# Three engines in program order instead of one, with the work dealt in smaller steps, in an attention and SwiGLU kernel

## The chip, the cores and the metric

The kernel runs on one core of a Trainium2 chip. The metric is device time in microseconds (us) from start to end of one execution; the median of the runs is taken. Nothing else runs on the core.

## The reference

```python
def _attn_ref(q, k, v):                 # 8 batches, 8 heads, 576 tokens, 64 values a head
    chunk, scale = 64, 1.0 / np.sqrt(64)
    q_c, k_c, v_c = (a.reshape(8, 8, 9, chunk, 64) for a in (q, k, v))
    scores = scale * np.matmul(q_c, k_c.transpose(0, 1, 2, 4, 3))
    scores = scores - np.max(scores, axis=-1, keepdims=True)
    attn = np.exp(scores)
    attn = attn / (np.sum(attn, axis=-1, keepdims=True) + 1e-09)
    return np.matmul(attn, v_c).reshape(8, 8, 576, 64)

def _moe_ref(x, w_gate, w_val, w_out, rms_g):   # x 4608 x 512; up to 1536, back to 512
    rms = np.sqrt(np.mean(x * x, axis=-1, keepdims=True) + 1e-06)
    xn = x / rms * rms_g
    g = xn @ w_gate
    silu = g * (1.0 / (1.0 + np.exp(-g)))
    return silu * (xn @ w_val) @ w_out
```

Each chunk of 64 tokens attends to itself. The heads are laid side by side to 4608 tokens of 512 values; these go through a norm and a gated up- and out-projection.

## The kernel before

The tokens go through in nine tiles of 512. Every operand of a projection is split into a high part (a copy rounded to the type that TensorE takes in one pass, on ScalarE) and a low part (operand less high part, on VectorE), and each product is the sum of three: high by high, high by low, low by high. So a matmul of 128x512 stands on TensorE for each of the three, and a split costs one ScalarE and one VectorE instruction.

**Tiles zero to two** are plain. In each, a loop over 12 feature blocks f makes the gate and the value product of block f (`up`, twelve matmuls each, L505), SiLU on ScalarE, the product with the value on VectorE, the split (`gated`), and then the out-projection of the block before (`down`, twelve matmuls, L540). In tiles one and two `half()` runs one step of a table of side work before `down` and one behind it.

**Tiles three to eight** are three pairs of tiles. A pair's projections use a scheme with seven block products P1 to P7 where eight would be due. `up_pair` runs for i = 0 to 5 over the seven products, each of two halves m (twelve matmuls together, L722); `after` turns the results into the gated block g: additions on VectorE, SiLU and copies on ScalarE, sums and products on GpSimd. Behind the seven, VectorE makes the operand tt and updates g in place (L761, L762). Then `down_pair` multiplies with the out weights in the order `DOWN`, each product for i = 0 to 5 (L911), with `finish` behind the last of a product. `split_next(n + 1)` splits the operand of the next product into gh and gl (L829, L830), one product ahead. The token operands of a pair (seven combinations of x, split as xp: L662, L663) are made by `x_sides`, the out weights of the seven products (side) by `out_sides` in tile two, the up weights' by `sides` in tile one; weights go through DRAM and come back through rings.

**The attention** of later tokens runs beside this, in units of 256 tokens, four to a pair of tiles (tile two carries the first pair's). From tile one on a unit (`unit_steps`) is: load q, k, v; scores (TensorE, L244) and softmax; the exponentials e turned in blocks of 32 by VectorE and stored to DRAM (away_e); read back as eT (L349); values (128 small matmuls of 64x64, L366); times the reciprocal sums rs, then the norm (squares summed on ScalarE, a power on GpSimd, a scale on ScalarE, L388); the result xu turned (L394) and stored (away_x); read back into x (L404). SyncE issues all of these transfers in one queue.

**What sets the order.** Work is dealt by tables: `UNIT_AT` and `UNIT_STEPS` in tile two, `PAIR_AT` and `PAIR_STEPS` in a pair give the step in which each part of a unit is emitted; `Steps` runs them. In tile zero a scheduler orders every engine. From tile one on TensorE runs in the order in which the code is written (`manual_schedule` with TensorE alone), while the scheduler still orders VectorE, ScalarE, GpSimd and SyncE: an instruction may be put ahead of others that are written before it, and `with urgent()` gives those on the path a priority. So the splits for the first products of an out-projection can be made long before it.

Of the kernel before, what the change touches and what calls it, by code (L numbers as in the profile page):

```python
# [17 lines left out]
P = 128  # L18
CH = 64
D = 64  # L20
H = 8
# [19 lines left out]
UNIT_STEPS = -2, 0, 1, 3, 5, 6, 7  # L41
FIRST_STEPS = -2, 0, 1, 3, 7, 8, 9
PAIR_STEPS = -4, 0, 3, 5, 8, 11, 13
PAIR_AT = 2, 12, 21, 31
# [24 lines left out]
def tile_chunk_attn_swiglu(  # L69
# [238 lines left out]
    def turned_softmax(i):  # L308
# [4 lines left out]
        for j in range(2):  # L313
            nc.vector.tensor_reduce(mx[:, j], st["s"][j], axis=AX.X, op=ALU.max)
            nc.vector.tensor_tensor(
                ev[:, j],
                st["s"][j].rearrange("p a (t k) -> p a t k", t=2),
                mx[:, j].rearrange("p a (o i) -> p a o i", i=1).broadcast_to([P, NPAIR, 2, Q]),
                op=ALU.subtract,
            )  # L320
        nc.scalar.activation(e, e, AF.Exp, scale=SCALE)
# [52 lines left out]
    def turned_norm(i):  # L374
        st = state.pop(i)
        if i % 2 == 0:

            state["xu", i // 2] = io.tile([P, 4, NDT, 2, Q], F32, tag="io", name="xu")
        xs = state["xu", i // 2].rearrange("p q a s d -> p s (q a) d")[:, i % 2]
        nc.vector.tensor_tensor(  # L380
            xs.rearrange("p (h b) d -> p h b d", b=2),
            st["o"].rearrange("p (h b d) -> p h b d", b=2, d=Q),
            st["rs"].rearrange("p h (o i) -> p h o i", i=1).broadcast_to([P, H, 2, Q]),
            op=ALU.mult,
        )

        spent = st["eT"].rearrange("p t h q -> p (t h) q")
        nc.scalar.mul(xs, xs, inv_rms(xs, spent))  # L388
# [125 lines left out]
    def gated(f, at, then):  # L514
# [14 lines left out]
        if 2 in at:  # L529
            then()  # L530
        with urgent():
# [41 lines left out]
    def out_sides(i, st):  # L573
# [6 lines left out]
        def join():  # L580
            w = st.tile([P, 2, DM], F32, tag="t1", bufs=1, name="wo")
# [75 lines left out]
    def x_side(p, src):  # L657

        t = xside[p] = big([P, 2, 2, TT], F32R, "xp")
        hi, lo = (t[:, i].rearrange("p k (n c) -> p k n c", c=2 * Q) for i in range(2))  # L660
        src = src.rearrange("p n k c -> p k n c")
        nc.scalar.copy(hi, src)  # L662
        nc.vector.tensor_tensor(lo, src, hi.bitcast(F32), op=ALU.subtract)  # L663

    xside = {}

    def x_sides(x1, x2, st):
# [3 lines left out]
        sub = ALU.subtract  # L671

        def scale(x, dts):
            for dt in dts:
                col = g_col[:, dt : dt + 1]
                nc.vector.tensor_scalar(x[:, :, dt], x[:, :, dt], col, None, op0=ALU.mult)

        def less(out, one, two):
            nc.vector.tensor_tensor(out, one, two, op=sub)

        def side_t1(p):
            x_side(p, got["t1"])

        def t1_first():
# [3 lines left out]
        got = {}  # L688
        first = [
            lambda: scale(x1, (0, 1)),  # L690
            lambda: scale(x1, (2, 3)),
        ]
        return first, [
            lambda: x_side(P1, b11),
            lambda: x_side(P2, b21),
            lambda: scale(x2, (0, 1)),
            t1_first,
            lambda: side_t1(P5),
            lambda: scale(x2, (2, 3)),
            lambda: less(got["t1"], b22, got["t1"]),  # L700
            lambda: side_t1(P6),
            lambda: x_side(P3, b22),
            lambda: less(b12, b22, b12),
            lambda: x_side(P7, b12),
            lambda: less(b21, got["t1"], b21),
            lambda: x_side(P4, b21),
        ]

# [116 lines left out]
    def split_g(src):  # L825
        gh = gp.tile([P, TT], F32R, name="gh")
        gl = gp.tile([P, TT], F32R, name="gl")
        with urgent():
            nc.scalar.copy(gh, src)  # L829
            nc.vector.tensor_tensor(gl, src, gh.bitcast(F32), op=ALU.subtract)  # L830
        return gh, gl

# [6 lines left out]
    def down_pair(t, gts, wos, step, more):  # L839
# [5 lines left out]
        def split_next(n):  # L845
            if n >= len(order):
                return
            p, i = order[n]
            g, tt = gts[i]
            src = {  # L850
# [3 lines left out]
            ready[n] = split_g(src)  # L854
# [11 lines left out]
        def finish(p, banks, kept):  # L866
            for m in range(2):
# [7 lines left out]
                elif p == P2:  # L875
                    o = tmp_tile("o")
# [18 lines left out]
        split_next(0)  # L895
        for n, (p, i) in enumerate(order):
# [9 lines left out]
            split_next(n + 1)  # L906
            gh, gl = ready.pop(n)
            w = wos[n // PER][:, n % PER]
            for k, (a, b) in enumerate(((0, gh), (1, gh), (0, gl))):
                for m in range(2):  # L910
                    nc.tensor.matmul(  # L911
                        banks[m][name],
                        w[:, a, m * P : (m + 1) * P],
                        b,
                        start=opens and i == 0 and k == 0,
                        stop=not (opens and p != P4) and i == NPR - 1 and k == 2,
                        skip_group_check=True,
                    )
            if i == NPR - 1:
                with urgent():  # L920
                    finish(p, banks, kept)
            step()

    def unit_steps(u, x):
# [3 lines left out]
        def first():  # L928
# [3 lines left out]
            for i in both:  # L932
                turned_softmax(i)

        def second():
            for i in both:
                turned_sum(i)
                turn(i)

        def third():  # L940
# [3 lines left out]
        def fourth():  # L944
            turned_values(u)
            for i in both:
                turned_norm(i)
# [5 lines left out]
            third,  # L953
            fourth,
# [54 lines left out]

    for t in range(PLAIN):  # L1010
        if t == 1:
            ordered = tc.manual_schedule(engines={mybir.EngineType.PE})
            ordered.__enter__()
            at = {}
# [3 lines left out]
            half = Steps(at)  # L1018
# [141 lines left out]
```

## Time and profile before

| | |
|---|---|
| runs | 930.78, 933.69, 937.71 us; median 933.69 |
| the profiled execution | 935.86 us; span of its instructions 934.0 us |
| granted TensorE clock, mean | 0.993 |
| TensorE / VectorE / ScalarE / GpSimd busy | 892.4 / 637.0 / 470.8 / 186.7 us |
| HBM traffic | 247 GB/s over the span |
| tiles zero and one | 0 to 258.4 us |
| tile two | 258.4 to 375.8 us |
| pair one: up, out | 375.8 to 505.8, to 567.0 us |
| pair two: up, out | 567.0 to 694.3, to 755.0 us |
| pair three: up, out (no attention beside it) | 755.0 to 870.6, to 934.0 us |

A row of the windows below gives a stretch, its length, the busy time of TensorE (with the number of instructions), its weight loads, VectorE, ScalarE, GpSimd, then the granted clock (1 is full), the share of the DMA engines and GB/s. A row of the timeline gives start, duration, engine, line, operation, result<-operands, tile, count, and in brackets how long the engine had waited and what ended the wait. SPq is SyncE's queue. Line numbers of the profile before are those of the kernel above; those of the changed kernel are other ones, since it has lines more.

### The profile page before, as it was taken

What the parts mean: (1) busy time and instruction counts of PE and PEld (TensorE: products, weight loads), DVE (VectorE), ACT (ScalarE), POOL (GpSimd) and SP (SyncE); (2) the same over time, 40 slices, a digit from 0 to 9 for tenths busy, and PEclk for the clock granted to TensorE, in tenths of its full rate; (3) what the DMA queues carried; (4) which work ended last, traced back from release to release, by engine and by line L of the source; (5) the groups of instructions that cost most, each with busy time, mean ns of one, the idle gap of its engine ahead of it and who ended that gap; (6) DMA issues with size and microseconds to landing.
All of it is one profiled execution on the core that took longest, in us unless ns stands there. A gap on an engine that the chain in (4) does not pass through costs nothing.

```text
span 934.0 us, 17571 instructions
## 1 busy us (share of the span) xinstructions
PE 892.4 (96%) x6828; PEld 726.1 (78%) x6828; DVE 637.0 (68%) x1065; ACT 470.8 (50%) x779; POOL 186.7 (20%) x161
## 2 busy tenths in 40 slices
PE   5699989999999989999998999999999999999997
PEld 4478868888888778888886888888877888888786
DVE  5899983654578783975775996666859954333775
ACT  4989853443456543744453654354636632322453
POOL 0100012224300000143333001443320013332201
PEclk9999999999999999999999999999999999999999
DMA  8688998778876766677796686777777675345801
GB/s 343 243 316 303 331 325 281 244 252 249 294 288 230 229 183 202 250 276 262 237 323 241 240 331 210 283 260 241 267 273 258 241 273 229 135 153 206 340 23 69
DMA packets 85795, 231.85 MB, mean 248 GB/s; under 512 B 8912, under 2 KB 45264, under 8 KB 71504
## 3 DMA queue, kind: packets, MB, share of 16 engines
q1 hardware_dynamic: 85712, 230.72, 70.3%
q8 instruction: 54, 0.88, 0.4%
q14 instruction: 29, 0.24, 0.1%
HBM read 167.25 MB, written 63.44 MB: 247 GB/s over the span
## 4 chain that ended last, share of the span: by engine, by line
PE 76%; issue 7%; ACT 6%; DVE 6%; POOL 2%; DMA 1%; SPq 0%; DVEq 0%; ACTq 0%; POOLq 0%
PE ps_c L722 11%; PE ps_a L722 11%; PE ps_b L722 10%; PE ps_g L505 7%; PE acc L540 7%; PE ps_v L505 7%; PE ps_b L911 5%; PE ps_d L722 5%; PE ps_c L911 4%; PE ps_d L911 3%; PE ps_a L911 3%; PE ps_o L366 2%; PE ps_s L244 2%; DVE gl L830 1%; ACT w L157 1%
## 5 line engine op out<-in xcount | busy, mean ns | idle before, releaser
L722 PE MATMUL ps_b<-xp,wr 128*128 128x512 f32 x432 | 106.0, 395 | 0.0
L722 PE MATMUL ps_c<-xp,wr 128*128 128x512 f32 x432 | 104.6, 391 | 0.0
L505 PE MATMUL ps_g<-xh,parts 128*128 128x512 f32 x288 | 98.1, 400 | 5.9 <-ACT sg L523 5.1
L722 PE MATMUL ps_a<-xp,wr 128*128 128x512 f32 x432 | 103.5, 390 | 0.0
L505 PE MATMUL ps_v<-xh,parts 128*128 128x512 f32 x288 | 96.0, 393 | 0.0
L722 PEld LDWEIGHTS ps_b<-xp,wr 128*128 128x128 f32 x432 | 81.7, 190 | 17.4
L722 PEld LDWEIGHTS ps_a<-xp,wr 128*128 128x128 f32 x432 | 80.9, 188 | 16.9
L722 PEld LDWEIGHTS ps_c<-xp,wr 128*128 128x128 f32 x432 | 80.6, 188 | 17.0
L540 PE MATMUL acc<-parts,gh 128*128 128x512 f32 x288 | 90.8, 396 | 0.0
L829 ACT CAST gh<-g 128x512 fp32r<-128x512 f32 x72 | 44.6, 623 | 51.8 <-DVE gl L830 21.0
L505 PEld LDWEIGHTS ps_g<-xh,parts 128*128 128x128 f32 x288 | 55.0, 191 | 19.5 <-ACT sg L523 6.4
L505 PEld LDWEIGHTS ps_v<-xh,parts 128*128 128x128 f32 x288 | 54.7, 190 | 11.5
L540 PEld LDWEIGHTS acc<-parts,gh 128*128 128x128 f32 x288 | 53.5, 189 | 11.6 <-ACT parts L182 0.2
L801 POOL TENSOR_TENSOR g<-u,u 128x512 f32<-128x512 f32 x18 | 23.2, 1289 | 185.8 <-ACT u L769 72.1
L830 DVE TENSOR_TENSOR gl<-g,gh 128x512 fp32r<-128x512 f32 x72 | 49.3, 700 | 12.2 <-ACT gh L829 11.9
L505 PE MATMUL ps_g<-xl,parts 128*128 128x512 f32 x144 | 57.0, 396 | 0.0
L540 PE MATMUL acc<-parts,gl 128*128 128x512 f32 x144 | 56.4, 392 | 0.0
L505 PE MATMUL ps_v<-xl,parts 128*128 128x512 f32 x144 | 56.4, 392 | 0.0
L791 POOL TENSOR_TENSOR p<-p,p 128x512 f32<-128x512 f32 x36 | 46.9, 1318 | 42.8 <-DVE p L790 33.5
L769 ACT ACTIVATE p<-p 128x512 f32<-128x512 f32 x36 | 22.6, 632 | 64.4 <-POOL p L791 61.2
L433 POOL TENSOR_TENSOR ri<-ss,mhalf 128x1 f32<-128x1 f32 x32 | 19.6, 623 | 173.6 <-DVE ss L431 173.5
L527 DVE TENSOR_TENSOR sg<-ps_v,sg 128x512 f32<-128x512 f32 x36 | 24.7, 686 | 42.0 <-PE ps_v L505 35.0
(141 smaller groups left out, 1794.9 us busy)
## 6 DMA issues: line engine op xcount, KB each, us to landing
wr<-wsd SPq DMA_DIRECT2D x63, 1024.0 KB, 6.8
wo<-osd SPq DMA_DIRECT2D x30, 1024.0 KB, 7.8
raw<-w_up_dram SPq DMA_DIRECT2D x12, 1024.0 KB, 9.6
vt<-v_dram SPq DMA_DIRECT2D x18, 512.0 KB, 5.2
wsd<-parts SPq DMA_DIRECT2D x18, 512.0 KB, 7.0
qt<-qT_dram SPq DMA_DIRECT2D x17, 512.0 KB, 4.9
kt<-kT_dram SPq DMA_DIRECT2D x17, 512.0 KB, 5.8
away_e<-e SPq DMA_DIRECT2D x28, 256.0 KB, 2.4
```

Of the source, the lines that this page charges most:

```text
L244: nc.tensor.matmul(st["s"][j][c * CH : (c + 1) * CH, pr], st["q"][rows, pr, tok : tok + CH], st["k"][rows, pr, tok : tok + CH], start=True ...
L433: nc.gpsimd.tensor_tensor(ri, ss, mhalf, op=ALU.pow)
L505: nc.tensor.matmul(ps, a[f][:, cols], b[dt], start=(dt == 0 and i == 0), stop=(dt == NDT - 1 and i == 2),)
L527: nc.vector.tensor_tensor(sg, pv, sg, op=ALU.mult)
L540: nc.tensor.matmul(acc[s], a[:, cols], b, start=(f == 0 and i == 0), stop=(f == NF - 1 and i == 2),)
L722: nc.tensor.matmul(ps, w[:, a, m, cols], xp[:, b, kt], start=start and kt == 0 and i == 0, stop=stop and kt == 1 and i == 2, skip_group_ch ...
L769: nc.scalar.activation(t, t if src is None else src, AF.Silu)
L791: nc.gpsimd.tensor_tensor(kp["p5"], kp["p1"], kp["p5"], op=add)
L801: nc.gpsimd.tensor_tensor(g[:, 0, 1], kp["u2"], kept[0]["u2"], op=mult)
L829: nc.scalar.copy(gh, src)
L830: nc.vector.tensor_tensor(gl, src, gh.bitcast(F32), op=ALU.subtract)
L911: nc.tensor.matmul(banks[m][name], w[:, a, m * P : (m + 1) * P], b, start=opens and i == 0 and k == 0, stop=not (opens and p != P4) and i ...
```

## The change

From tile two on TensorE, ScalarE and VectorE run in the order in which the code is written (`IN_ORDER`); GpSimd and SyncE keep the scheduler. A unit has eleven steps in place of seven: the softmax of the two halves, the exponentials, the turns, the norm, its root and its scale are steps of their own, and the power of both halves is one instruction on two columns. The token operands are made in more and smaller steps, their scale by rms_g goes from VectorE to ScalarE, and those of the last four products (P3, P6, P7, P4) are split in the first steps of the stage that uses them. Three of the six `out_sides` move from tile two to tile one. In tile two a step runs between gh and gl (`between`). In `down_pair` gh is made two products ahead and gl one, and the last of each product finishes its half m = 0 first.

```diff
+PAIR_AT = 3, 12, 22, 31
+PAIR_STEPS = -4, 0, 1, 3, 4, 5, 8, 9, 10, 11, 13
+UNIT_STEPS = -2, 0, 0, 1, 1, 3, 5, 6, 6, 7, 8
+IN_ORDER = {mybir.EngineType.PE, mybir.EngineType.Activation, mybir.EngineType.DVE}
...
+    def turned_norm(u):
...
+            nc.scalar.activation(spent, xv[:, s], AF.Square, accum_out=ss[:, s : s + 1])
+    def turned_root(u):
+        ss = state["ss", u]
+        nc.vector.tensor_scalar(ss, ss, 1.0 / DM, 1e-6, op0=ALU.mult, op1=ALU.add)
+        ri = state["ri", u] = small.tile([P, 2], F32, name="ri_u")
+        nc.gpsimd.tensor_tensor(ri, ss, mhalf.broadcast_to([P, 2]), op=ALU.pow)
+    def turned_scale(u):
...
+            nc.scalar.mul(xv[:, s], xv[:, s], ri[:, s : s + 1])
...
+        if between is not None:
+            between()
         with urgent():
             nc.vector.tensor_tensor(gl, sg, gh.bitcast(F32), op=ALU.subtract)
...
-                nc.vector.tensor_scalar(x[:, :, dt], x[:, :, dt], col, None, op0=ALU.mult)
+                nc.scalar.mul(x[:, :, dt], x[:, :, dt], col)
...
+        late = [
+            [lambda: less(got["t1"], b22, got["t1"]), lambda: high(P3), lambda: high(P6)],
+            [lambda: low(P6), lambda: less(b12, b22, b12), lambda: low(P3), lambda: high(P7)],
+            [lambda: low(P7), lambda: less(b21, got["t1"], b21), lambda: high(P4)],
+            [lambda: low(P4)],
+        ]
...
-        with urgent():
-            nc.scalar.copy(gh, src)
-            nc.vector.tensor_tensor(gl, src, gh.bitcast(F32), op=ALU.subtract)
...
+        def split_high(n):
+            if n < len(order):
+                gh = tmp.tile([P, TT], F32R, tag="tmp", name="gh")
+                nc.scalar.copy(gh, source(n))
+                ready[n] = [gh]
...
+        def split_low(n):
...
+            gl = gp.tile([P, TT], F32R, name="gl")
+            nc.vector.tensor_tensor(gl, source(n), ready[n][0].bitcast(F32), op=sub)
...
-        split_next(0)
+        split_high(0)
+        split_high(1)
+        split_low(0)
...
-            split_next(n + 1)
+            split_high(n + 2)
+            split_low(n + 1)
...
-            for k, (a, b) in enumerate(((0, gh), (1, gh), (0, gl))):
-                for m in range(2):
...
+            todo = [(m, k) for k in range(3) for m in range(2)]
             if i == NPR - 1:
-                with urgent():
-                    finish(p, banks, kept)
+                todo.sort()
+            for m, k in todo:
...
+            for i in range(OUT_FIRST):
+                for k, f in enumerate(out_sides(i, st, "ab", 3)):
+                    at.setdefault(7 + 6 * i + k, []).append(f)
...
+            ordered.__exit__(None, None, None)
...
+            ordered = tc.manual_schedule(engines=IN_ORDER)
+            ordered.__enter__()
...
+            g = gated(f, CONVS[f % 2], conv_step, half if t == 2 else None)
```

**VectorE around the first pair's out-projection.** Before, in row order; the first piece lies inside the up stage, the second at its end. p1 less ps_d is the end of P4 (two halves), g<-g is the update of the last block, xu is the last unit's turn, gl are the low parts of the out-projection's operands, the number behind the name tells the tiles apart (g_4026 is the block of i = 0, g_4227 of i = 1, g_4503 of i = 2).

```order
L762 TENSOR_TENSOR g_4026<-g_4026 128x512
L830 TENSOR_TENSOR gl_5474<-g_4026,gh_5473 128x512
L778 TENSOR_TENSOR u2_4294<-ps_b_4280,p1_4242 128x512
L778 TENSOR_TENSOR u2_4296<-ps_b_4287,p1_4244 128x512
L784 TENSOR_TENSOR g_4227<-ps_a_4235,c11_4312 128x512
L830 TENSOR_TENSOR gl_5482<-g_4227,gh_5481 128x512
```

```order
L803 TENSOR_TENSOR p1_5269<-p1_5269,ps_d_5453 128x512
L762 TENSOR_TENSOR g_5254<-g_5254 128x512
L394 STREAM_TRANSPOSE xu_5418<-xu_5418 128x1024
L803 TENSOR_TENSOR p1_5271<-p1_5271,ps_d_5460 128x512
L830 TENSOR_TENSOR gl_5495<-g_4503,gh_5494 128x512
L663 TENSOR_TENSOR xp_5568<-x_127,xp_5568 128x1024
L830 TENSOR_TENSOR gl_5505<-g_4750,gh_5504 128x512
```

The same place in the changed kernel, whose blocks i = 0, 1, 2 are g_3989, g_4199, g_4475 and whose gl is L881:

```order
L829 TENSOR_TENSOR p1_5225<-p1_5225,ps_d_5414 128x512
L829 TENSOR_TENSOR p1_5227<-p1_5227,ps_d_5421 128x512
L787 TENSOR_TENSOR tt_5207<-g_5210 128x512
L788 TENSOR_TENSOR g_5210<-g_5210 128x512
L881 TENSOR_TENSOR gl_5440<-g_3989,gh_5436 128x512
L881 TENSOR_TENSOR gl_5448<-g_4199,gh_5438 128x512
L411 STREAM_TRANSPOSE xu_5385<-xu_5385 128x1024
L881 TENSOR_TENSOR gl_5461<-g_4475,gh_5446 128x512
L881 TENSOR_TENSOR gl_5471<-g_4716,gh_5459 128x512
```

The low parts of i = 0 and i = 1 have moved from the up stage to behind P4's two halves, tt and the update of g.

**ScalarE at the same place.** p5 and p1 are SiLUs (P7, P4), xu<-xu,ri the scale of the norm, gh the high parts, xp a token operand. Before:

```order
L769 ACTIVATE p5_5289<-p5_5289 128x512
L388 ACTIVATE xu_5418<-xu_5418,ri_5423 128x16x32
L388 ACTIVATE xu_5418<-xu_5418,ri_5430 128x16x32
L769 ACTIVATE p1_5269<-p1_5269 128x512
L662 CAST xp_5568<-x_127 128x1024
L829 CAST gh_5494<-g_4503 128x512
L829 CAST gh_5504<-g_4750 128x512
```

In the changed kernel:

```order
L795 ACTIVATE p5_5256<-p5_5256 128x512
L795 ACTIVATE p1_5225<-p1_5225 128x512
L405 ACTIVATE xu_5385<-xu_5385,ri_u_5410 128x16x32 x2
L874 CAST gh_5436<-g_3989 128x512
L874 CAST gh_5438<-g_4199 128x512
L874 CAST gh_5446<-g_4475 128x512
```

The first two gh, made in the up stage before, now stand behind P4's SiLU and the two scales.

**SyncE's queue in tile two**, at the third unit. e is stored to away_e and read back as eT, x comes back from away_x of the unit before. Before:

```order
L349 DMA eT<-away_e_3320 32x2x256 x2
L397 DMA away_x_3358<-xu 128x1024
L349 DMA eT<-away_e_3320 32x2x256 x2
L349 DMA eT<-away_e_3327 32x2x256
L214 DMA vt<-v_dram 128x1024
L404 DMA x<-away_x_3358 32x4x256 x4
L349 DMA eT<-away_e_3327 32x2x256 x3
```

In the changed kernel:

```order
L355 DMA eT<-away_e_3361 32x2x256 x4
L355 DMA eT<-away_e_3368 32x2x256 x2
L414 DMA away_x_3433<-xu 128x1024
L355 DMA eT<-away_e_3368 32x2x256 x2
L217 DMA vt<-v_dram 128x1024
```

The four reads of x, which stood ahead of the last three of eT, come behind all eight now.

More of the change, by code (lines that the diff above doesn't have):

```diff
@@ L512, in up, with gated @@
         return ps
-    def gated(f, at, then):
+    def gated(f, at, then, between=None):
         pg = up(wgh, wgl, f, "ps_g")
@@ L670, in x_sides, with views, high, low @@
         b11, b21, b12, b22 = x1[:, :, :2], x1[:, :, 2:], x2[:, :, :2], x2[:, :, 2:]
-        sub = ALU.subtract
+        got = {}
+        src = {P1: lambda: b11, P2: lambda: b21, P5: lambda: got["t1"], P6: lambda: got["t1"]}
+        src.update({P3: lambda: b22, P7: lambda: b12, P4: lambda: b21})
+        def views(p):
+            t = xside[p]
+            hi, lo = (t[:, i].rearrange("p k (n c) -> p k n c", c=2 * Q) for i in range(2))
+            return hi, lo, src[p]().rearrange("p n k c -> p k n c")
+        def high(p):
+            xside[p] = big([P, 2, 2, TT], F32R, "xp")
+            hi, _, x = views(p)
+            nc.scalar.copy(hi, x)
+        def low(p):
+            hi, lo, x = views(p)
+            nc.vector.tensor_tensor(lo, x, hi.bitcast(F32), op=ALU.subtract)
         def scale(x, dts):
@@ L931, in first, with second, away, back @@
                 scores(i, sc)
+            turned_softmax(both[0])
+        def second():
+            turned_softmax(both[1])
             for i in both:
[L933 to L940, printed above, removed]
+                turned_exp(i)
+        def away(i):
+            turned_sum(i)
+            turn(i)
+        def back():
             for i in both:
                 turn_back(i)
-        def fourth():
+        def values():
             turned_values(u)
-            for i in both:
-                turned_norm(i)
+            turned_norm(u)
         return [
@@ L952, in unit_steps @@
             second,
-            third,
-            fourth,
+            lambda: away(both[0]),
+            lambda: away(both[1]),
+            back,
+            values,
+            lambda: turned_root(u),
+            lambda: turned_scale(u),
             lambda: turn_x(u),
@@ L1095, in tile_chunk_attn_swiglu @@
                     at.setdefault(max(PAIR_AT[n] + PAIR_STEPS[k], 0), []).append(f)
-            first, both = x_sides(x, x2, st)
-            for n, f in enumerate(first):
-                at.setdefault(PAIR_AT[1] + PAIR_STEPS[-1] + 4 + n, []).append(f)
-            for n, f in enumerate(both):
-                at.setdefault(7 * NPR + 6 + 5 * n // 2, []).append(f)
+            one, two, late = x_sides(x, x2, st)
+            for n, f in enumerate(one[:2]):
+                at.setdefault(PAIR_AT[1] + PAIR_STEPS[-1] + 2 + n, []).append(f)
+            for n, f in zip(X_AT, one[2:] + two[:1] + two[4:] + two[1:4]):
+                at.setdefault(7 * NPR + n, []).append(f)
+            early = {n: list(todo) for n, todo in enumerate(late)}
         step = Steps(at)
```

148 lines of the change are left out of this document (69 added, 79 removed).

## The prediction

> **What bounds the kernel now.** I read the busy table, then TensorE's waits, then the timeline around each wait.
>
> ```profile
> PE 892.4 (96%) x6828; PEld 726.1 (78%) x6828; DVE 637.0 (68%) x1065; ACT 470.8 (50%) x779; POOL 186.7 (20%) x161
> ...
> 406.90 1.48 PE L366 MATMUL ps_o<-vt,eT 64*32 64x64 f32 x128
> 408.31 3.02 PE L722 MATMUL ps_c<-xp,wr 128*128 128x512 f32 x12
> 411.17 1.07 PE L722 MATMUL ps_b<-xp,wr 128*128 128x512 f32 x4
> ```
>
> TensorE has 96%, and no edit takes a matmul away. Twelve wide matmuls take 2.86 us here (408.31 to 411.17), 2.72 without the 0.14 of the switch, so 0.227 each; a burst of attention values takes 1.41 (406.90 to 408.31). The change can win or lose only what TensorE idles. Tiles zero and one keep their scheduler, so I look from 258 us on. Three losses stand there. **Tile two:**
>
> ```profile
> 258.40:375.80 117.40, 113.72 (x1202) 92.52 (x1202) 83.58 (x178) 60.04 (x101) 5.24 (x8) 0.99 0.69 221
> ...
> 307.85 0.27 PE L366 MATMUL ps_o<-vt,eT 64*32 64x64 f32 x2 [0.33 <-DMA eT<-away_e]
> 309.00 1.94 PE L366 MATMUL ps_o<-vt,eT 64*32 64x64 f32 x126 [0.88 <-DVE rs L326]
> 330.70 2.42 PE L366 MATMUL ps_o<-vt,eT 64*32 64x64 f32 x126 [1.55 <-DMA eT<-away_e]
> 337.34 0.50 PE L505 MATMUL ps_g<-xh,parts 128*128 128x512 f32 x1 [0.59 <-ACT sg L523]
> ...
> 327.57:330.98 3.41, 1.77 (x12) 1.00 1.11 277
> 330.98:334.40 3.42, 3.29 (x126) 0.52 0.64 231
> ```
>
> 36 groups of twelve (97.9 us) and four units of about 2.5 (10.0) are 107.9 of the 117.4, so 9.5 are lost. Waits with a name are 3.35: the eT tiles, which come back from DRAM late, and a late silu. After the idle window from 327.57 the next 3.42 us were granted 0.52 of the clock, which costs 1.6.
>
> **The start of each paired out-projection**, here pair two; the last up product begins at 691.55, the out-projection at 694.27:
>
> ```profile
> L829 ACT CAST gh<-g x2: 619/620/620, 573.3 to 599.1; 128x512 fp32r<-128x512 f32 x2
> L830 DVE TENSOR_TENSOR gl<-g,gh x2: 693/693/693, 573.9 to 599.7; 128x512 fp32r<-128x512 f32 x2
> ...
> 690.15 1.28 DVE L380 TENSOR_TENSOR xu<-ps_o,rs 128x512 f32<-128x512 f32 x2
> 691.55 2.88 PE L722 MATMUL ps_d<-xp,wr 128*128 128x512 f32 x12
> 693.97 1.32 ACT L388 ACTIVATE xu<-xu,ri 128x512 f32<-128x512 f32 x2
> 694.27 1.07 PE L911 MATMUL ps_a<-gh,wo 128*128 128x512 f32 x4
> 694.39 1.29 POOL L791 TENSOR_TENSOR p<-p,p 128x512 f32<-128x512 f32 x1
> 697.08 0.69 DVE L762 TENSOR_TENSOR g<-g 128x512 f32<-128x512 f32 x1 [2.97 <-POOL g L795]
> 697.69 1.24 DVE L394 STREAM_TRANSPOSE xu<-xu 128x1024 f32<-128x1024 f32 x1
> 699.43 0.68 DVE L830 TENSOR_TENSOR gl<-g,gh 128x512 fp32r<-128x512 f32 x1
> 700.16 0.74 PE L911 MATMUL ps_a<-gl,wo 128*128 128x512 f32 x2 [1.62 <-DVE gl L830]
> 702.99 0.74 PE L911 MATMUL ps_a<-gl,wo 128*128 128x512 f32 x2 [1.17 <-DVE gl L830]
> ...
> PE ps_a L911 <- DVE gl L830: 6.0, 7, 1.6
> ```
>
> The first two splits were made over 90 us ahead, in the up stage. The third comes only after VectorE has waited for GpSimd (697.08) and turned a tile (697.69). All such waits sum to 6.0; seven of them, about 0.17 longer from start to start (a matmul is booked 0.39 but spaced 0.227), make 7.2. **A stall with no engine behind it**, in the last burst of pair one, and the clock around it and around pair two's start:
>
> ```profile
> 498.52 0.31 PE L366 MATMUL ps_o<-vt,eT 64*32 64x64 f32 x1 [2.03 <-issue]
> ...
> 494.82:498.24 3.42, 1.67 (x129) 1.00 1.01 422
> 498.24:501.65 3.41, 3.13 (x8) 0.52 1.01 428
> ...
> 699.62:703.04 3.42, 1.72 (x7) 1.00 1.00 333
> ```
>
> With the half clock behind it this one costs 2.3 + 1.6 = 3.9.
>
> **The change part by part.** *Tile two in program order.* The eT pieces are no longer queued behind the four loads of x, which wait for their own DRAM trip; only the store away_x still stands between them. From the end of an up product E:
>
> ```profile
> L349 SPq DMA_DIRECT2D eT<-away_e x32: 302/425/1075, 273.1 to 344.2; - x32
> ...
> DMA to landing us min/median/max: 1.8/2.7/5.2
> ...
> L527 DVE TENSOR_TENSOR sg<-ps_v,sg 128x512 f32<-128x512 f32 x12 | 8.2, 684 | 12.2 <-PE ps_v L505 8.4 <-issue 3.7
> ```
>
> the product sg (0.7, perhaps 0.3 late), the turn (1.24, as at 697.69), four issues of about 0.42 and the landing (2.7) give E + 6.6, up to E + 9.1 with the longest landing. TensorE comes to the burst after a down product (2.72), scores (1.1) and an up product (5.44): E + 9.3; for the last unit, which has no scores ahead, E + 8.2. So the waits go with a margin of 1.6 to 2.7. I count -5.5: 3.35 of waits, 1.6 of clock, 0.5 of the bursts' slow flow; bounds -3.3 (waits alone) and -8.4 (all but the switches between kinds of matmul, 8 times 0.14).
>
> Three out_sides move to tile one:
>
> ```profile
> L598 DVE TENSOR_TENSOR side<-wo,side x24: 370/419/426, 277.0 to 360.2; 128x256 fp32r<-128x256 f32 x24
> ```
>
> each takes eight VectorE passes over 128x256, about 0.42 like this one, and one over 128x1024, by the token split's 1.2 below: 4.6. I found no stall in tile one with such work as its cause, and count 0. The squares' sum to the scale, one power for a pair instead of two, and the scale by g on ScalarE run beside matmuls; ScalarE is busy half of the time: 0, unless the power is long (rival three).
>
> *Splits further ahead.* gh is made two products ahead, but gl stays one ahead, and in program order the first gh and gl now come after all of the last up product. In pair two's times: the two norms end at 690.0 (values end 688.7, 1.28); the half m=0 of P7 ends 690.2, its sum on VectorE (0.69) 690.9; m=1 likewise 692.3. GpSimd:
>
> ```profile
> L433 POOL TENSOR_TENSOR ri<-ss,mhalf 128x1 f32<-128x1 f32 x24 | 13.8, 588 | 137.7 <-DVE ss L431 137.7
> L470 POOL TENSOR_TENSOR ri_u<-ss_u,mhalf x2: 1616/2779/3942, 83.5 to 126.6; 128x2 f32<-128x2 f32 x2
> L769 ACT ACTIVATE p<-p 128x512 f32<-128x512 f32 x36 | 22.6, 632 | 64.4 <-POOL p L791 61.2 <-DVE p L803 2.3
> ...
> 398.63 1.29 POOL L807 TENSOR_TENSOR g<-p,p 128x512 f32<-128x512 f32 x1
> 398.69 1.78 DVE L762 TENSOR_TENSOR g<-g 128x512 f32<-128x512 f32 x1
> ```
>
> two sums of 1.3 to 693.6, the power to 694.2 (0.59, nearest to the 24 rows of this stage; 3.9 is the other end), the product to 695.5. ScalarE: silu of P4 to 694.25, the two scales (1.32) to 695.6, the first gh (0.62) to 696.2. TensorE, due at 694.27, starts 2.0 late and has four matmuls (0.9) until it needs gl, at 697.15. VectorE: P4's second half to 695.0, tt to 695.7, then the update of g. GpSimd takes up its next product in the same moment, and with that beside it this update took 1.78 at 398.69: 697.45; the first gl ends 698.1, another 0.95 late. Together 3.0. Pair three has no unit, no scales: gh 0.7 late, gl 1.7 more, 2.4. So -7.2 go and 3.0 + 3.0 + 2.4 = +8.4 come (bounds: 4.5 if GpSimd's next product waits and gh is early; 11 if the turn that follows adds its 1.24 as well).
>
> And the clock: a window with 1.77 or 1.67 us busy of 3.41 was followed by 0.52, one with 1.72 was not (699.62). A stall of 2.0 and one of 0.95 within 3.9 us leave a window about half idle in some 3 of 4 positions. I take it in pairs one and two: +3.2 (0 to 4.8). [...]
>
> *Pair starts in the up stage.* P6's low part must now be ready at 8.4 after the first product:
>
> ```profile
> L663 DVE TENSOR_TENSOR xp<-t,xp 128x1024 fp32r<-128x1024 f32 x6 | 7.3, 1218 | 0.0
> ```
>
> the second product ends at 5.44, silu 0.6, the product g 0.7, the split 1.2: 7.95. It fits by 0.45; +0.5 for three pairs (0 to 1.5).
>
> *The last out-projection finishes m=0 three matmuls earlier:*
>
> ```profile
> 928.42 0.61 PE L911 MATMUL ps_d<-gl,wo 128*128 128x512 f32 x2
> 928.92 1.29 DVE L890 TENSOR_TENSOR p<-p,ps_d 128x512 f32<-128x512 f32 x2 [1.67 <-PE ps_d L911]
> ```
>
> so only one of the two subtractions stands behind the last matmul: -0.6.
>
> *The stall at 498* belongs to TensorE's own stream, which is nearly the same: no row says whether it falls on the burst again. Half of 3.9, -1.9 (0 to -3.9).
>
> **Sum**, on the profiled span of 934.0: -5.5 - 7.2 + 8.4 + 3.2 + 0.5 - 0.6 - 1.9 = -3.1, so 930.9; its execution took 935.86, 1.9 more. The median shown is 933.69, less 3.1: **930.6**.
>
> **Rivals.** [...] *Two, the starts are cheap:* if gh and gl come with the lower bound of 4.5 and no half clock, tile two gives all 8.4 and the stall at 498 goes, the sum is -8.4 - 7.2 + 4.5 - 0.6 - 3.9 = -15.6: 918. For it: only GpSimd's order makes the update late. Against: VectorE waited 2.97 for that product before. *Three, slower: the power over two columns takes 3.9*, as once at 126. ScalarE, in order, then stands 3.3 longer ahead of the scale: both starts +6.6; in tile two the silu behind it comes about 1 late in each of four units, +4; copies of P1 in the up stage, +2: 943. It decides from about 2 us on. Against it: no single power took over 1.1 from 258 on. *Four, slower: eT lands after 9.3:* 2 us late and a half clock each in four units, 14.4 in place of the waits gone, 930.6 + 5.5 + 14.4 = 950; it needs landings over 5.4, and 5.2 was the longest. *Five, the order leads as before* and tile two keeps its waits: 936.
>
> **How the numbers follow.** Forecast 0.40, rival one 0.15, two 0.25, three 0.07, four 0.04, five 0.09. Within 1% (924.4 to 943.0, about what a measurement of this kernel can tell from no change) lie the forecast, one and five, less 0.05 for forecasts with the 498 stall gone and two cheap starts: 0.58. Faster 0.30, slower 0.12 (three lies on the border). The range, 918 to 940, leaves out three and four and half of two.
>
> **What would show it.** In the profile after: no eT wait in tile two; a wait of about 2 on gh and about 1 on gl at each out-projection's first products; VectorE's update of g waiting for GpSimd just ahead; a window at 0.52 behind it; the tail 0.6 shorter. The forecast is wrong if the first gl is ready when the out-projection starts, if powers take over 2 us, or if values still wait.

## The result: 5% slower

The changed kernel takes 983.3 us (median of 977.08, 981.23, 985.36 and 987.09) against 933.77: a ratio of 1.051, 95% interval 1.0474 to 1.0547. The forecast was 930.6, its range ended at 940. The profiled execution is the fastest of the four (977.08).

The busy table of the changed kernel, then three windows of TensorE alone: tile one before, then tiles one and two of the changed kernel. A row gives the stretch, its length, TensorE's busy time with the number of matmuls, the granted clock, DMA share and GB/s:

```profile
PE 903.4 (93%) x6828; PEld 733.5 (75%) x6828; DVE 645.4 (66%) x1027; ACT 463.7 (48%) x787; POOL 180.0 (18%) x147
```

```profile
154.30:258.10 103.80, 103.80 (x818) 1.00 0.79 255
149.70:271.20 121.50, 110.23 (x818) 0.94 0.76 243
271.20:395.30 124.10, 114.41 (x1202) 0.96 0.60 192
```

TensorE has the same 6828 matmuls, and no other engine is busy more than 8.4 us longer; the time is idle time and half clock (windows of 3.41 that were granted 0.50 to 0.53). The stages from first matmul to first matmul, in us, of every kernel run here (one profiled execution each; pair three with the tail; tile zero took 150 to 156 in all of them and is left out, 149.7 in the changed kernel, 154.3 before):

| | median / before of its runs | tile one | tile two | pair one | pair two | pair three |
|---|---|---|---|---|---|---|
| before | 933.77 | 103.8 | 117.3 | 191.3 | 189.6 | 177.5 |
| changed | 983.3 / 933.77 | 121.5 | 124.1 | 201.3 | 197.3 | 181.2 |
| e2, all out_sides in tile two | 973.83 / 934.43 | 103.8 | 130.8 | 203.2 | 198.6 | 181.3 |
| e5, gl ahead of the step | 975.51 / 934.43 | 120.6 | 117.8 | 206.4 | 197.9 | 179.6 |
| e3, PAIR_AT as before | 976.98 / 934.43 | 121.9 | 125.0 | 200.3 | 191.8 | 180.8 |
| e6, both halves away at once | 990.06 / 936.41 | 119.5 | 125.8 | 210.0 | 199.3 | 180.9 |
| e7, first splits early | 980.17 / 936.41 | 124.0 | 124.9 | 201.8 | 195.8 | 179.0 |
| e8, scheduler | 955.61 / 936.41 | 120.7 | 111.5 | 197.3 | 190.0 | 177.0 |
| e10, stores on GpSimd's queue | 982.8 / 933.81 | 125.2 | 119.9 | 203.2 | 199.3 | 180.7 |
| e9, five edits, program order | 958.73 / 936.41 | 103.8 | 129.9 | 200.8 | 189.4 | 178.6 |
| e14, three edits and scheduler | 941.46 / 935.47 | 103.9 | 119.2 | 196.0 | 189.2 | 177.5 |
| e4, before with the new PAIR_AT | 943.66 / 934.43 | 103.9 | 117.9 | 199.2 | 190.4 | 177.3 |
| e11, before in program order | 992.93 / 933.81 | 103.8 | 132.1 | 218.8 | 201.1 | 182.8 |
| e12, before, 28 matmuls twice | 941.21 / 933.81 | 103.8 | 117.9 | 195.9 | 189.9 | 176.9 |
| e13, before, two edits | 934.11 / 933.81 | 103.8 | 116.5 | 190.0 | 190.8 | 176.9 |
| e15, before, out_sides moved | 944.27 / 935.47 | 120.4 | 113.6 | 189.3 | 188.6 | 177.0 |

Each run has a median of the kernel before from its own session; these medians differ by up to 2.6, so a difference between two rows of the table can carry as much. Against before the changed kernel loses 17.7 in tile one, 6.8 in tile two, 10.0 and 7.7 in pairs one and two, 3.7 in pair three. With 4.6 gained in tile zero that is the 41.3 between the two profiled executions; the medians lie 49.5 apart. Four places in its timeline show how.

**Tile one.** TensorE, ScalarE and SyncE's queue at the longest stall:

```profile
235.47 0.60 ACT L540 ACTIVATE sg<-ps_g 128x512 f32<-128x512 f32 x1 [7.09 <-DMA osd<-side]
228.95 0.32 SPq L645 DMA_DIRECT2D w<-wfd  x1
229.32 3.24 SPq L355 DMA_DIRECT2D eT<-away_e  x7
232.66 1.85 SPq L620 DMA_DIRECT2D osd<-side  x4
236.12 0.80 PE L522 MATMUL ps_g<-xh,parts 128*128 128x512 f32 x1 [6.40 <-ACT sg L540]
```

The SiLU sg needs one of the four tmp buffers, and all hold pieces of an out_side, whose stores stand in SyncE's queue behind a load of w and seven reads of eT. So TensorE waits 6.4 for a buffer; the next matmul then takes 0.80 in place of 0.39, in a window granted 0.50 (234.26 to 237.68). With 2.8 on a load of kt and 2.0 on the product sg TensorE waits 11.2 in this tile, and four windows of 3.41 granted 0.50 (from 203.54, 234.26, 237.68 and 261.57) cost some 6.7: together the 17.7. Before it has neither here.

**Tile two.** ScalarE, VectorE and TensorE at the fourth piece of an out_side:

```profile
314.70 1.01 ACT L616 CAST side<-wo 128x256 fp32r<-128x256 f32 x3
321.85 0.40 ACT L616 CAST side<-wo 128x256 fp32r<-128x256 f32 x1 [6.13 <-DMA osd<-side]
322.62 0.68 DVE L551 TENSOR_TENSOR gl<-sg,gh 128x512 fp32r<-128x512 f32 x1
325.25 0.42 DVE L318 TENSOR_TENSOR e<-ps_s,mx 128x256 f32<-128x256 f32 x1
325.78 0.27 PE L372 MATMUL ps_o<-vt,eT 64*32 64x64 f32 x2 [4.59 <-issue]
```

and the clock window behind it:

```profile
326.29:329.70 3.41, 3.13 (x128) 0.52 0.75 214
```

The step now stands between gh and gl. gl still has to read sg, so three buffers are left for four pieces, and the fourth waits for the store of the first. In program order VectorE's gl and the next unit's softmax stand behind it, and the values need the banks that this softmax reads: TensorE starts 0.1 after its end. Before, no order held gl behind the pieces.

**The pairs, scores behind values.** TensorE's rows:

```profile
438.58 0.46 PE L247 MATMUL ps_s<-kt,qt 64*64 64x64 f32 x16
440.51 0.93 PE L247 MATMUL ps_s<-kt,qt 64*64 64x64 f32 x48 [1.47 <-issue]
...
502.01 0.68 PE L247 MATMUL ps_s<-kt,qt 64*64 64x64 f32 x29 [2.37 <-issue]
```

Nothing releases TensorE here. The new PAIR_AT puts the scores of the second and the fourth unit one product (2.7) behind the values of the unit before, where two stood between them. There are five such stalls, 8.1 us in all: four in these scores, and one in the values of pair one's last unit, where before the only one of 2.0 lay.

**The start of the out-projections**, here pair two, then pair three, with the clock windows around them:

```profile
731.53 1.33 ACT L405 ACTIVATE xu<-xu,ri_u 128x512 f32<-128x512 f32 x2
732.68 1.74 POOL L833 TENSOR_TENSOR g<-p,p 128x512 f32<-128x512 f32 x1
733.38 1.59 DVE L788 TENSOR_TENSOR g<-g 128x512 f32<-128x512 f32 x1
733.43 1.20 PE L946 MATMUL ps_a<-gh,wo 128*128 128x512 f32 x4 [1.97 <-ACT gh L874]
735.62 0.90 PE L946 MATMUL ps_a<-gl,wo 128*128 128x512 f32 x2 [1.00 <-DVE gl L881]
...
909.11 1.20 PE L946 MATMUL ps_a<-gh,wo 128*128 128x512 f32 x4 [0.66 <-ACT gh L874]
912.19 0.73 PE L946 MATMUL ps_a<-gl,wo 128*128 128x512 f32 x2 [1.88 <-DVE gl L881]
```

```profile
732.48:735.89 3.41, 1.46 (x5) 1.00 0.61 257
735.89:739.30 3.41, 3.41 (x9) 0.52 0.33 133
...
913.38:916.80 3.42, 3.42 (x11) 0.52 1.02 426
```

This is the chain of the forecast: gh behind the two scales, gl behind the update of g, which takes 1.59 with GpSimd's next product beside it (0.69 at 697.08 before, with nothing of GpSimd's beside it). One sign is missing: VectorE does not wait for GpSimd ahead of this update.

### The profile page after: what moved, and what is told of

It is laid out like the page before. It is cut to its first block, busy times and chain, and to the rows that moved or that the text cites. A ratio compares the mean times of both kernels' runs of the same rounds, so it can differ in the third digit from the quotient of the medians.

```text
span 975.3 us, 17521 instructions
## 1 busy us (share of the span) xinstructions
PE 903.4 (93%) x6828; PEld 733.5 (75%) x6828; DVE 645.4 (66%) x1027; ACT 463.7 (48%) x787; POOL 180.0 (18%) x147
## 4 chain that ended last, share of the span: by engine, by line
PE 50%; DVE 17%; DMA 11%; issue 9%; ACT 8%; SPq 2%; POOL 2%; DVEq 0%; ACTq 0%; POOLq 0%
PE ps_b L748 7%; PE ps_a L748 7%; PE ps_c L748 6%; PE ps_a L946 5%; PE ps_b L946 5%; PE ps_c L946 5%; PE ps_d L748 4%; DMA wsd<-w 2%; PE ps_g L522 2%; PE ps_v L522 2%; PE acc L559 2%; DMA away_e<-e 2%; PE ps_d L946 2%; DMA eT<-away_e 2%; PE ps_o L372 2%
## 5 line engine op out<-in xcount | busy, mean ns | idle before, releaser
L522 PE MATMUL ps_g<-xh,parts 128*128 128x512 f32 x288 | 100.1, 407 | 9.4 <-ACT sg L540 8.6
L881 DVE TENSOR_TENSOR gl<-g,gh 128x512 fp32r<-128x512 f32 x72 | 49.1, 687 | 24.8 <-PE ps_a L946 9.5
L748 PE MATMUL ps_d<-xp,wr 128*128 128x512 f32 x216 | 52.2, 390 | 0.0
```

What stands on the lines that cost most here:

```text
L522: nc.tensor.matmul(ps, a[f][:, cols], b[dt], start=(dt == 0 and i == 0), stop=(dt == NDT - 1 and i == 2),)
L748: nc.tensor.matmul(ps, w[:, a, m, cols], xp[:, b, kt], start=start and kt == 0 and i == 0, stop=stop and kt == 1 and i == 2, skip_group_ch ...
L881: nc.vector.tensor_tensor(gl, source(n), ready[n][0].bitcast(F32), op=sub)
```

## The experiments

### Tile one and the buffers

```diff
-OUT_FIRST = 3
+OUT_FIRST = 0
...
-                    at.setdefault(3 + 4 * n + k // 2, []).append(f)
+                    at.setdefault(3 + 3 * n + k // 2, []).append(f)
```

> The changed kernel with all six out_sides in tile two again (steps 3 + 3n + k//2, so that their splits fall on steps 4, 7, 10, 13, 16, 19), none in tile one. Theory A (tile one loses its 17.7 us because the pieces of out_sides fill the four tmp buffers and sg waits for their stores): tile one comes back to the kernel before, about -17; in tile two the split stalls ScalarE for 5 to 7 us only where it stands between gh and gl (steps 4, 10, 16: three waits for osd stores, as now), not on steps 7, 13, 19. Time about 966. Rival B (what counts is the amount of VectorE work, 4.6 us for each, wherever it stands): tile two loses what tile one wins, time 978 to 985, and waits for stores do not follow the step's parity.

Measured 973.83 (1.0403, 1.0354 to 1.0452). The window of tile one, then ScalarE in tile two:

```profile
154.00:257.80 103.80, 103.80 (x818) 1.00 0.80 255
```

```profile
301.46 1.31 ACT L616 CAST side<-wo 128x256 fp32r<-128x256 f32 x4
306.05 0.60 ACT L540 ACTIVATE sg<-ps_g 128x512 f32<-128x512 f32 x1 [3.28 <-DMA osd<-side]
...
324.48 0.41 ACT L616 CAST side<-wo 128x256 fp32r<-128x256 f32 x1 [5.06 <-DMA osd<-side]
```

Tile one is back at its 103.8, without any idle time. In tile two the fourth piece waits at steps 4, 10 and 16 (2.33, 5.06, 3.83), and at steps 7, 13 and 19 all four pieces run at once: the parity that theory A demands. A had not foreseen that at the odd steps the wait comes just behind the pieces, at the next sg or the table load ahead of it (3.28, 2.19, 1.44). So the pieces' stores are waited for at all six steps, and the parity decides only who waits. Tile two grows by 6.7, so a part comes back.

The opposite test moves the three out_sides alone, on the kernel before:

```diff
+            for i in range(3):
+                for k, f in enumerate(out_sides(i, st, "ab", 3)):
+                    at.setdefault(7 + 6 * i + k, []).append(f)
...
-            for i in range(NPR):
+            for i in range(3, NPR):
                 for k, f in enumerate(out_sides(i, st)):
```

> The kernel before with three of the six out_sides in tile one (steps 7 + 6i + k, in the buffers of sides), the others in tile two as they were. If this edit alone costs tile one its time: tile one 12 to 18 longer, tile two up to 5 shorter, 942 to 949. If it needed the smaller steps or program order behind it: 930 to 936.

Measured 944.27 (1.0086, 1.0058 to 1.0115). The window of tile one, and TensorE in it:

```profile
153.50:273.90 120.40, 107.85 (x818) 0.96 0.73 234
```

```profile
206.12 1.37 PE L244 MATMUL ps_s<-kt,qt 64*64 64x64 f32 x64 [3.09 <-DMA kt<-kT_dram]
240.81 0.80 PE L505 MATMUL ps_g<-xh,parts 128*128 128x512 f32 x1 [7.24 <-ACT sg L523]
```

The move alone costs tile one 16.6 and gives tile two 3.7, and the stalls are those of the changed kernel. This edit needs no program order to do harm: VectorE and ScalarE are ordered by the scheduler in tile one in all these kernels. The other candidate was SyncE's queue:

```diff
-                nc.sync.dma_start(out_home(i, p), part.rearrange("p a c -> p (a c)").bitcast(F32))
+                nc.gpsimd.dma_start(out_home(i, p), part.rearrange("p a c -> p (a c)").bitcast(F32))
```

> The changed kernel with the stores of out_sides (osd<-side) issued on GpSimd's queue in place of SyncE's, nothing else. Theory A2 (the four tmp buffers stay taken because the stores stand in SyncE's queue behind reads that wait): tile one loses little against the kernel before (under 5 in place of 17.7), the waits on osd stores in tile two fall from 15.2 to under 6; time 960 to 970. Rival (it is the landing or the count of buffers): less than 6 us gained, 977 or more.

Measured 982.8 (1.0518): the rival is right. ScalarE's waits ahead of the pieces in the whole run, then the issues of the stores with their KB and us to landing:

```profile
  DMA osd<-side: 16.0, 4
```

```profile
osd<-side POOLq DMA_DIRECT2D x24, 256.0 KB, 5.1
```

The stores no longer queue behind SyncE's reads, but land after 5.1 (2.9 from SyncE's queue in tile one, 3.6 in tile two). The wait of 7.09 on sg shrinks to 2.6, but others come, and tile one takes 125.2; of the 15.2 that the pieces wait in tile two 11.4 stay. So the queue alone is not the cause. That the moved out_sides cost tile one its time is shown, by e2 and e15. That it goes by the four buffers is read from the rows; whether more of them, or an earlier landing, would do away with the waits was not tried.

### The step between gh and gl

```diff
-            g = gated(f, CONVS[f % 2], conv_step, half if t == 2 else None)
+            g = gated(f, CONVS[f % 2], conv_step)
...
+            if t == 2:
+                half()
             if prev is not None:
                 down(acc, f - 1, *prev)
```

> The changed kernel with the step of tile two behind gl again (before the out-projection of the block), not between gh and gl; out_sides as in the changed kernel. Theory A (the split of four pieces stands ahead of the gl that reads sg, so that three of the four tmp buffers are left, and the fourth piece waits for the store of the first, with ScalarE and VectorE in program order behind it): the three waits of 15.2 us in all on osd stores in tile two go, the gaps of 4.8 and 4.3 on TensorE ahead of the attention values with them, and the half clock behind them (about 4): about -12, 971. Rival B (the stores are late because of SyncE's queue, whatever stands on ScalarE): the waits stay, 980 to 986.

Measured 975.51 (1.0429, 1.0381 to 1.0476). What ScalarE waited for ahead of the pieces (L616), in the whole run, us and times; first the row on stores of the changed kernel, then all rows of this run:

```profile
  DMA osd<-side: 15.2, 3
```

```profile
  DVE wo L597: 8.1, 3
  DMA wsd<-side: 3.1, 3
  DVE gl L551: 0.8, 1
```

No piece waits for an osd store any more (the table load behind them does, 2.8 in all), and tile two falls from 124.1 to 117.8. A's mechanism holds; its size was too high, as a new wait of 3.9 came at one burst of scores. And pair one is 5.1 longer in this profile, which is not explained.

### Program order

```diff
-IN_ORDER = {mybir.EngineType.PE, mybir.EngineType.Activation, mybir.EngineType.DVE}
+IN_ORDER = {mybir.EngineType.PE}
```

> The changed kernel with IN_ORDER reduced to TensorE: the same steps and tables, but VectorE and ScalarE ordered by the scheduler from tile two on, as before. Theory G (the loss sits in where the steps stand and what shares a buffer, and the program order only passes each late instruction on to those behind it): tile one keeps its 17 us and the bursts in the pairs their stalls, while waits in tile two and at the starts shrink to a part: 955 to 970. Rival (program order itself is the cause): 935 to 945. Third possibility (the scheduler without the priorities that the change removed does worse): over 985.

Measured 955.61 (1.0223, 1.0187 to 1.0259): 27.7 below the changed kernel. By the table it wins 12.6 in tile two, 4.0, 7.3 and 4.2 in the pairs, and 0.8 in tile one. The reverse puts VectorE and ScalarE of the kernel before into program order:

```diff
+            ordered.__exit__(None, None, None)
...
             half = Steps(at)
+            ordered = tc.manual_schedule(engines={mybir.EngineType.PE, mybir.EngineType.Activation, mybir.EngineType.DVE})
+            ordered.__enter__()
```

> The kernel before with VectorE and ScalarE in program order from tile two on, nothing else: its large steps, its splits one ahead. Theory G2 (program order costs, since what stands late in the program passes its wait on; the smaller steps were needed for it): slower than the kernel before by 40 or more, 975 to 1010, with long waits at the three starts and behind each unit. Rival (the small steps and moved pieces are what costs, program order little): 934 to 950.

Measured 992.93 (1.0624, 1.0592 to 1.0656), so program order alone costs 59 there. TensorE's longest waits:

```profile
PE ps_a L722 <- ACT p L775: 11.1, 1, 11.1
...
PE ps_c L911 <- DVE gl L830: 5.1, 6, 1.2
```

The 11.1 stands at pair one's start, where the copy of P1 must wait on ScalarE behind casts of token operands that themselves wait for VectorE. In the three out-projections the waits on gh and gl come to 18.9, against 6.2 before. This is what theory G2 names, though the longest wait is at another start. The changed kernel with five edits comes to 958.7 in program order (e9 below), 34 under e11. So its other parts, smaller steps among them, help in program order, but they do not make up for it; the smaller steps alone were not run.

### Bursts one product apart

```diff
-PAIR_AT = 3, 12, 22, 31
+PAIR_AT = 2, 12, 21, 31
```

> The changed kernel with PAIR_AT = 2, 12, 21, 31 in place of 3, 12, 22, 31. Theory C (a burst of attention values one product ahead of a burst of scores takes two stretches of TensorE's instructions within 4 us, and the second is not there yet): the stalls without an engine in the scores of units 1 and 3 of each pair (1.7 and 2.6, 0.7 and 1.65 us) go, because values and scores there are two products apart again; at most one such stall comes at unit 2's scores. About -6, 976. Rival D (where a stall falls is set by how the instructions lie in the stretches alone): as many stalls of the same kind elsewhere in the bursts, 980 to 986.

On the kernel before, the reverse:

```diff
-PAIR_AT = 2, 12, 21, 31
+PAIR_AT = 3, 12, 22, 31
```

> The kernel before with PAIR_AT = 3, 12, 22, 31 in place of 2, 12, 21, 31, nothing else. Theory C: stalls without an engine come in the scores of units 1 and 3 of pairs one and two, 1 to 2.6 us each, some with a half clock behind them: +5 to +8, about 940. Rival D: no more such stalls than the one that it has, 931 to 936.

Measured 976.98 (1.0442), 6.3 below the changed kernel; and 943.66 (1.0092, 1.0066 to 1.0118), 9.2 above the kernel before. TensorE in the second:

```profile
415.40 0.81 PE L244 MATMUL ps_s<-kt,qt 64*64 64x64 f32 x40 [1.29 <-issue]
474.97 0.69 PE L244 MATMUL ps_s<-kt,qt 64*64 64x64 f32 x29 [1.36 <-issue]
506.04 0.31 PE L366 MATMUL ps_o<-vt,eT 64*32 64x64 f32 x1 [5.26 <-issue]
```

Three of the four stalls in scores that theory C names came (the third, at 672, of 1.22), and in e3 all four were gone. One stall is in both that C doesn't name: the last unit's values of pair one, 4.7 and 5.3 of idle time here, 2.0 and 2.4 in the two kernels of the case. So of the 9.2 some 3.9 are the stalls in scores and 3.2 the growth of this one. To see whether it is the place in the instruction stream, 28 small matmuls were added ahead of it:

```diff
+                    if i in (20, 21) and 4 * pr + 2 * j + c < 14:
+                        nc.tensor.matmul(
+                            st["s"][j][c * CH : (c + 1) * CH, pr],
...
```

> The kernel before with 28 of the small score matmuls of the first unit of pair one made twice (same operands, same result), which shifts all later instructions of TensorE by 56. In every run so far the stalls without an engine lie at instruction number 192 or 193 modulo 256, counted over TensorE's matmuls, weight loads and semaphore instructions, where 256 of them pass in less than some 4 us. Theory C2 (it is this count): the stall of 2.25 us at 496 (last unit of pair one) goes with the half clock behind it, and one of 2 to 5 us comes at about 598 in the values of the first unit of pair two, where a stretch of 256 now falls on one burst; time within 4 of the kernel before. Rival (the stall belongs to that unit's data or its place in the stage): it stays at 496 and none comes at 598.

Measured 941.21 (1.0079, 1.0054 to 1.0104). The stall at 496 is gone, as C2 says, but none came at 598; others came, the longest in a product behind a burst of values:

```profile
474.42 2.19 PE L730 MATMUL ps_b<-xp,wr 128*128 128x512 f32 x6 [2.79 <-issue]
```

So the stall moved with the count. The shift is some 112, though, not the 56 of the expectation: in the kernel before the trace has 1,152 matmuls at L244 for 576 calls, so the 28 are 56 matmuls with 56 weight loads. The matmul that resumes at 474.42 stands at 85 modulo 256 there, the one at 498.52 at 194; and the place at 598 rested on the 56. That a stall falls where 256 instructions pass in under 4 isn't shown either: in the kernel before they passed in 2.63 at 195, without one. The shift alone, with no burst moved against another, costs 7.4 where at most 4 was expected. e3 and e4 move the spacing and the count together, so how much of their 6 to 9 is the spacing that theory C names isn't shown.

### Units and starts

```diff
-PAIR_STEPS = -4, 0, 1, 3, 4, 5, 8, 9, 10, 11, 13
+PAIR_STEPS = -4, 0, 1, 3, 3, 5, 8, 9, 10, 11, 13
```

> The changed kernel with both halves of a unit's exponentials turned and stored in the same step of a pair (PAIR_STEPS with 3, 3 in place of 3, 4); the step of the read back (5) and of the values (8) stay. Theory E (the second half, turned one step later, stands behind the VectorE work at the end of a block, so that the store, the read back and with them eT come late at the values): the waits on eT in the pairs, about 4.8 us, and the half clock behind the one at 633 go: about -6, 977. Rival (SyncE's eight issues of 0.64 us and the landing set the time): eT stays late, 981 to 985.

Measured 990.06 (1.0585, 1.0558 to 1.0612), slower still: theory E falls. The waits on eT in the whole run, first of the changed kernel, then of this one:

```profile
PE ps_o L372 <- DMA eT<-away_e: 5.8, 8, 1.6
```

```profile
PE ps_o L372 <- DMA eT<-away_e: 7.3, 10, 1.9
```

Two waits on weights came too (3.2), and the stall in pair one's last unit grew from 2.4 to 4.2. What did help the units is e3, where the first and the third unit stand one step earlier: the blocks with the first unit's values take 22.0 (from 26.5 and 27.1). Why the smaller shift hurt is open.

```diff
+            if i == NPR - 1 and k == 6:
+                first_splits(gts)
```

> The changed kernel with the first two gh and gl of each paired out-projection made ahead of the last up product (P4 of i = 5), all else as it is. Theory F (in program order the first splits stand behind the scales, P4's sums, tt and the update of g): the waits of 9.5 us on gh and gl at the three starts go or shrink below 3, and the half clocks behind them (three of 1.6) go: -9 to -14, about 971. Rival (the third split, still behind the update of g, is late in place of the first): waits of 1 to 2 on gl remain in each pair, about 977.

Measured 980.17 (1.0476, 1.0445 to 1.0508). TensorE at pair one's start:

```profile
543.25 1.07 PE L955 MATMUL ps_a<-gh,wo 128*128 128x512 f32 x4
...
547.00 1.19 PE L955 MATMUL ps_a<-gh,wo 128*128 128x512 f32 x4 [0.87 <-ACT gh L886]
```

and its waits at the three starts:

```profile
PE ps_a L955 <- DVE gl L893: 3.2, 3, 1.1
PE ps_a L955 <- ACT gh L886: 2.5, 3, 0.9
```

The first two, gh and gl, are ready; the third, still behind the chain, is late in their place: 5.7 in all. The rival described it. The interval overlaps that of the changed kernel, so no gain is shown.

### Together

e9 holds the five edits of e2, e5, e3, e6 and e7, program order kept.

> Five edits together on the changed kernel, program order kept: all out_sides in tile two, the step behind gl, PAIR_AT = 2, 12, 21, 31, both halves away in one step, and the first two splits ahead of the last up product. If the causes named so far are the whole of the loss, they add up to -17, -6, -6, -6 and -12, with 3 given back by the fuller tile two: 983 - 44 = about 939. If they hide one another or something else holds: 950 or more. If program order is worth something once the stalls are gone: below 930.

Measured 958.73 (1.0237, 1.0202 to 1.0271): 20 above the 939 of the sum, but not because the edits hide one another. Alone e2, e5, e3 and e7 gave 9.5, 7.8, 6.3 and 3.1 and e6 took 6.8, in medians, which makes 20.0; together they give 24.6 (both are 27.2 when each run is set against the kernel before of its own session). The sizes put into the sum were too high. Stage by stage they do not add: tile two still takes 129.9 with six out_sides in program order, where e5 alone had 117.8, while the pairs gain more than alone. A stall of 5.3 stands in pair one. The same without program order and without e6 and e7:

> The changed kernel with the scheduler for VectorE and ScalarE (IN_ORDER with TensorE alone), all six out_sides in tile two, the step of tile two behind gl, and PAIR_AT = 2, 12, 21, 31. If the causes add: 955.6 - 17 (tile one) + 5 (six out_sides in tile two) - 6 (bursts apart) = about 938, level with the kernel before within 1%. If the smaller steps and later operands are worth something under the scheduler: 925 or less. If they cost by themselves: 945 or more.

Measured 941.46 (1.0057, 1.0036 to 1.0079): within 1% of the kernel before, near the sum. Last, the kernel before with what the readings suggested, UNIT_STEPS ending in 8 and 12 small matmuls made twice:

> The kernel before with two edits: in tile two x is read back one step later (UNIT_STEPS with 8 at the end), so that all eight reads of eT stand ahead of the four reads of x in SyncE's queue; and 12 small score matmuls made twice in pair one's first unit, the shift at which no 256 instructions of TensorE pass in less than 4 us. If the readings hold: the waits on eT of 2.6 us in tile two and the half clock there go (-4), and the stall at 496 with its half clock (-3 to -4): about 926. If the two are hidden by something else: 931 to 935.

Measured 934.11 (0.9997, 0.9976 to 1.0018): level. The stall at 496 is gone, and 0.3 is left of the eT waits in tile two. But a silu wait of 2.8 and one of 1.4 on kt stand in tile two, and two new stalls without an engine (1.1 and 0.6) in pair two. No version here beats the kernel before.

## Why the prediction was wrong, by its own steps

- **Three out_sides in tile one: 0.** This step failed first. I looked for VectorE's time there and found room; what ran out, by the rows above, were the four tmp buffers. Alone the move measures +16.6 in tile one and -3.7 in tile two (e15).
- **Tile two: -5.5.** Measured +6.8. The part on eT held: no wait on it is left there (0.5 in e5, where the values are not held up by the softmax). But I had weighed only what SyncE's queue does, and not that the step between gh and gl takes a buffer that gl must free, on an engine that may not go on (e5: 6.3 of it; program order in all 12.6, e8). Nor is the -5.5 there otherwise: with the scheduler and six out_sides tile two takes 119.2, as a silu wait of 5.1 stands there (e14).
- **The new PAIR_AT was not priced at all.** It is in the diff, and the forecast has no term for it. Alone it costs 9.2 on the kernel before (e4) and gives 6.3 when taken back (e3).
- **The stall at 498: -1.9.** It stayed, and four more came: 8.1 for 2.0. The half clock behind it did go (1.00 was granted from 357.1 to 538.0).
- **The values in pairs one and two: no term.** I asked for eT in tile two alone. In the pairs TensorE waits 5.8 on it in eight places, where before it has no such wait, and a window granted 0.52 follows one of them (from 633.49). Under the scheduler 0.3 is left (e8). Which instruction makes eT late there isn't shown; e6 speaks against the one that I suspected.
- **The starts: -7.2 and +8.4.** Right: 1.96 + 1.00, 1.97 + 1.00 and 0.66 + 1.88 are 8.47, with the engines that I named, save that the update of g was slow beside GpSimd (1.59) and did not wait for it.
- **The clock: +3.2 for two half windows.** There are three, 4.8: pair three has one too. No idle piece there was longer than 1.97: 1.96 and 1.00, 1.97 and 1.00, 0.66 and 1.88, in windows that were busy for 1.20, 1.46 and 1.53 of 3.41. The window behind each was granted 0.52.
- **Pair starts: +0.5.** Pair one has one wait, of 1.59, on the copy of P1; the others none. Small, but for another reason: P6's low part, which I had priced, was in time.
- **The tail: -0.6.** From the last matmul's start to the end it fell from 5.3 to 4.9.
- **The power over two columns** (rival three): its median is 0.70, its longest from 197 on 1.60. It decided nothing.

By stage the forecast was off by 17.7 in tile one, 12.3 in tile two and 19.0 in the pairs. One slip of addition: the chances named for a time within 1% make 0.59, not 0.58. Forecast and rivals missed the mechanism that I asked about only at the starts: in program order a wait goes to everything behind it. e8 puts 27.7 of the 49.5 there, e2 and e15 put 9 to 10 on the out_sides (16.6 lost in tile one, a part back in tile two), e3 and e4 6 to 9 on PAIR_AT. These overlap, and e14, without all of them, is 6 us above the kernel before.

## What to carry to other kernels

Before an engine goes into program order, list for each moved instruction the buffer that it takes, and what must run to free it; if that comes late or stands behind it, the engine waits, here for a store (15.2 in tile two). Price a moved step by the buffers and queue places that it takes, not only by its engine's free time. And price every number of a table that moves: a unit one step later (9.2 in e4) changed what stands next to what on TensorE, and where it lies in TensorE's count of instructions.

## What the hardware showed

Stalls of TensorE inside a burst of small matmuls, with no engine behind them, stood at nearly one count. Counted over matmuls, weight loads and semaphore instructions, the first matmul after the stall before (498.52) stands at 194 modulo 256, those after the five of the changed kernel (440.51, 502.01, 528.51, 640.29, 700.94) at 193 or 194; in these six the matmuls sit idle for 0.49 to 2.40 us. Over the traces of all kernels here I counted 48, at 192 to 194, of 0.3 to 5.3 us, those behind a burst included. In the two traces of the case one transfer of kind instruction, 16 KB, begins 2.2 to 2.6 us ahead of each of the six resumptions. The page of the changed kernel lists them, with MB and share:

```profile
q8 instruction: 54, 0.88, 0.4%
```

These 54 stand against 13,851 TensorE instructions, 256.5 for each. From the first of the 256 ahead of a stall to the resumption it took 3.8 us before and 4.4 to 7.1 in the changed kernel, stall included. Speed alone does not decide: in the kernel before 256 passed in 2.63 at 195 with no stall, in the changed kernel in 2.63 at 191. What starts such a transfer isn't shown.
